# Turning B and C of eight chunk pairs on VectorE instead of TensorE, in a fused Mamba-2 and PReLU kernel

## The chip, the cores and the metric

The kernel runs on one NeuronCore of a Trainium2 chip. The metric is the device time of one execution in microseconds, the median over several runs. The core has five engines that run side by side, each through its own list of instructions in order: TensorE (PE in the profile; PEld is its loading of weights), VectorE (DVE), ScalarE (ACT), GpSimd (POOL) and SyncE (SP), which here issues most of the transfers between the main memory and the on-chip memory SBUF. Matmul results land in PSUM. An engine waits for another through semaphores.

## The reference

Two blocks follow each other. The first is a Mamba-2 state-space scan in chunks, the second a dense layer with PReLU.

```python
# x: (4, 8, 768, 32)   a: (4, 8, 768)   B, C: (4, 8, 768, 16)    float32
log_a = np.log(np.clip(a, 1e-06, 1.0))
for c in range(nc):                                  # chunks along the sequence
    cum  = np.cumsum(la, axis=-1)
    L    = np.exp(cum[:, :, :, None] - cum[:, :, None, :]) * causal
    CB   = np.einsum('bhin,bhjn->bhij', Cc, Bc)      # products of C and B
    M    = CB * L
    y_intra = np.einsum('bhij,bhjd->bhid', M, xc)
    y_inter = np.einsum('bhin,bhnd->bhid', Cc, state) * np.exp(cum)[:, :, :, None]
    y[:, :, sl] = y_intra + y_inter
    state = decay_full[:, :, None, None] * state + np.sum(Bx, axis=2)   # Bx from B, x, decay
# ...
x = attn_out.transpose(0, 2, 1, 3).reshape(3072, 256)
h = x @ w_in                                         # w_in: (256, 2048)
g = np.maximum(h, 0.0) + alpha * np.minimum(h, 0.0)
out = g @ w_out                                      # w_out: (2048, 256)
```

## The kernel before

The kernel works in chunks of Q = 128 positions, two chunks at a time: a *pair*, gp = 0 to 11. Two pairs fill a group of 512 tokens, which the dense layer then takes. The dense layer of group 1 onwards is done in *quads* of four row blocks, `quad(g, z, after)`, by a scheme of seven products with sums and differences of blocks in place of eight products. Between its steps a quad calls `after(1)` to `after(14)`, and there the parts of the next group's pairs are put in. So the state-space work of pairs 4 to 11 is spread through the matmuls of the dense layer, in an order that is fixed in the program.

Loading a pair. `nat` has B and C with positions on the partitions, and (head, state) along the row:

```python
nat = ldx.tile([P, 2, 2, H * N], F32, name="nat")
# ...
for k in range(2):
    ts = slice((c + k) * Q, (c + k + 1) * Q)
    for i, src in enumerate((B, C)):
        eng = nc.scalar if gp == 0 else nc.sync
        eng.dma_start(out=nat[:, i, k].rearrange("p (h n) -> p h n", h=H),
                      in_=src[b, :, ts, :].rearrange("h p n -> p h n"))      # L163
    nc.sync.dma_start(out=xt[:, k]..., in_=x[b, :, ts, :]...)                # L165
```

A pair's work, for the last eight pairs (`fine`, gp >= 4). The products of B and C need (head, state) on the partitions, so both are turned:

```python
# ... bn (B times decays, from nat[:, 0]), state update; yield
tp = spare() if gp == 1 else ss_tile()                       # a PSUM tile
for i in range(2):
    for k in range(2):
        nc.tensor.transpose(tp[:, (2 * i + k) * P : (2 * i + k + 1) * P], nat[:, i, k],
                            ident)                           # L511
bc = work.tile([P, 4, Q], F32, name="bc")
nc.scalar.copy(out=bc.rearrange("p i t -> p (i t)"), in_=tp) # L514
bh, ct = bc[:, :2], bc[:, 2:].rearrange("p k t -> p (k t)")
# ...
yield
for k in range(2):                   # each half_decays: two scans of 256 columns, L441
    for w in range(2):
        half_decays(k, w)
        if k == 1 and w == 1:
            spread_c()               # ScalarE: cz from ct, L526
            c_decayed()              # GpSimd: cd from ct, L529
        yield
# ... products of bh and cz (L580), times the decays (L614), y (L633, L640), copy to xT
```

A quad's steps (`first` is a group of four matmuls, L785; A and Y are PSUM tiles of a pool of two):

```python
first(A, lambda q: wi[:, q, 0, 0], b11, True)
m1 = ...; nc.scalar.copy(out=m1, in_=A)                          # L793
after(1)
first(Y, lambda q: s1[:, q], t1, True)
m5 = ...; nc.scalar.copy(out=m5, in_=Y)                          # L797
after(2); after(3)
first(A, lambda q: s2[:, q], t2)
u2 = ...; nc.scalar.copy(out=u2, in_=A)                          # L802
after(4)
nc.vector.tensor_tensor(out=Y, in0=Y, in1=u2, op=ALU.add)        # L804
after(5)
first(A, lambda q: wi[:, q, 1, 0], t3)
c22 = ...; nc.vector.tensor_tensor(out=c22, in0=A, in1=m5, op=ALU.add)   # L808
after(6)
first(Y, lambda q: s4[:, q], b22)          # accumulates on what L804 left in Y
prelu(g12, Y, z, 0)                        # ScalarE multiply L768, VectorE L770
prelu(g22, c22, z, 1, (nc.scalar,))
nc.scalar.copy(out=Y, in_=m1)                                    # L814
prelu(g22, c22, z, 1, (nc.vector,))
after(7); after(8)
# ... g21 from A
first(Y, lambda q: wi[:, q, 0, 1], b21)
prelu(g11, Y, z, 0)                        # the quad's last PReLU
# ... GpSimd differences of the g blocks, L828
after(11); after(12); after(13); after(14)
```

A pair's turning of B and C is called at `after(12)` of an odd quad (z = 1 or 3), its first two scans at `after(14)`, the next four at `after(1)` and `after(2)` of the following quad, and the last two at its `after(5)`. Pair 4 alone has its first parts, the turning and two scans among them, ahead of the first quad. From group 2 on, `after(11)` of an odd quad has `finish`, which turns one half of the output of the group before with a VectorE block transpose (L904) and stores it. The products with `w_out` (L760; in the first quads also L699) stand between the steps.

Of the kernel before, what the change touches and what calls it, by code (L numbers as in the profile page):

```python
# [9 lines left out]
F32 = mybir.dt.float32  # L10
# [12 lines left out]
def kernel(  # L23
# [25 lines left out]
    nc = tc.nc  # L49
# [4 lines left out]
    batch, H, S, D = x.shape  # L54
    N = B.shape[-1]
    P = 128
    Q = 128
# [8 lines left out]
    GC = 4  # L66
# [20 lines left out]
    ldx = ctx.enter_context(tc.tile_pool(name="ldx", bufs=3))  # L87
# [5 lines left out]
    gp = ctx.enter_context(tc.tile_pool(name="gp", bufs=16))  # L93
# [6 lines left out]
    def bank(i):  # L100


        return ps_q.tile([P, 512], F32, name="bank", tag=f"q{i}")
# [5 lines left out]
    def ss_tile():  # L109
        if early[0] is None:  # L110
            return ps_s.tile([P, 512], F32, name="ss")
        early[0] += 1
        i = early[0] % (3 if ident_p else 4)
        return ps_s.tile([P, 512], F32, name="ss") if i < 2 else bank(i)
# [4 lines left out]
    def load_rows(i):  # L119

        rows = ld.tile([RW, Q], F32, name="rows")
        nc.sync.dma_start(out=rows, in_=a.rearrange("b h (c t) -> (b h c) t", t=Q)[i * RW : (i + 1) * RW])
        loads["r", i] = rows
# [3 lines left out]
    def load_a(t, b, c, eng=nc.sync):  # L127
        first = a[b, 0:1, c * Q : (c + 2) * Q]
        eng.dma_start(out=t, in_=bass.AP(tensor=first.tensor, offset=first.offset,
                                             ap=[[S, H], [0, N], [1, 2 * Q]]))  # L130

    def load_spread(gp, b, c):

        for k, t in enumerate(loads["p", gp][1]):
            rows = scratch["z", b // 2].rearrange("(b h c) t -> b c h t", b=2, h=H)[b % 2, c + k]
            nc.sync.dma_start(out=t.rearrange("p (h t) -> p h t", h=H),
                              in_=rows.unsqueeze(0).to_broadcast([P, H, Q]))

    def load_pair(gp, decays=True):


        b, c = divmod(2 * gp, CPB)
        nat = ldx.tile([P, 2, 2, H * N], F32, name="nat")
        xt = ldx.tile([P, 2, HD], F32, name="xt")

        ap = ldx.tile([P, 2 * Q], F32, name="ap")
        if gp == 0:
            load_a(ap, b, c, nc.scalar)
        elif gp >= NB:
            rows = scratch["pf", b // 2].rearrange("(b h c) t -> b h (c t)", b=2, h=H)  # L150
            rows = rows[b % 2, :, c * Q : (c + 2) * Q]
            nc.sync.dma_start(out=ap, in_=rows.unsqueeze(1).to_broadcast([H, N, 2 * Q]))
        if gp == 0:
            load_rows(0)
            nc.sync.dma_start(out=al_n, in_=moe_alpha.rearrange("(k p) -> k p", p=P))
            loads["a", 1] = prep.tile([P, 2 * Q], F32, name="a1")
            load_a(loads["a", 1], b, c + 2)
        abc = []
        for k in range(2):
            ts = slice((c + k) * Q, (c + k + 1) * Q)  # L160
            for i, src in enumerate((B, C)):
                eng = nc.scalar if gp == 0 else nc.sync
                eng.dma_start(out=nat[:, i, k].rearrange("p (h n) -> p h n", h=H),  # L163
                              in_=src[b, :, ts, :].rearrange("h p n -> p h n"))
            nc.sync.dma_start(out=xt[:, k].rearrange("p (h d) -> p h d", h=H),  # L165
                              in_=x[b, :, ts, :].rearrange("h p d -> p h d"))
        for k in range(2 if gp >= NB else 0):
            abc.append(lda.tile([P, H * Q], F32, name="abc"))
        loads["p", gp] = nat, abc, xt, ap
        if decays:  # L170
            load_spread(gp, b, c)
# [6 lines left out]

    al_n = const.tile([NF, P], F32, name="al_n")
    load_pair(0)  # L180

    w_in = const.tile([P, KC, d_ff], F32, name="w_in")
# [84 lines left out]
    def keep_warm(to, n, cols=2 * Q):  # L267

        for i in range(n):
            nc.tensor.matmul(to[:, :cols], warm[:, :P], warm[:, :cols], start=True, stop=True,  # L270
                             skip_group_check=True)

    keep_warm(ps_h.tile([P, GT], F32, name="hp"), 7, Q)
    ident = const.tile([P, P], F32, name="ident")
# [3 lines left out]
                          in_=ident.unsqueeze(1).to_broadcast([P, H, Q]))  # L278
# [135 lines left out]
    def spare():  # L414

        return ps_h.tile([P, GT], F32, name="hp", tag="hp")

    def pair(gp):

        b, c = divmod(2 * gp, CPB)  # L420
        nat, abc, xt, ap = loads["p", gp]
        last = c + 2 == CPB
        fine = gp >= 2 * GC // 2
# [79 lines left out]
            yield  # L503


        tp = spare() if gp == 1 else ss_tile()
        if gp == 0:
            keep_warm(tp, 3, Q)
        for i in range(2):
            for k in range(2):  # L510
                nc.tensor.transpose(tp[:, (2 * i + k) * P : (2 * i + k + 1) * P], nat[:, i, k],  # L511
                                    ident)
        bc = work.tile([P, 4, Q], F32, name="bc")
        nc.scalar.copy(out=bc.rearrange("p i t -> p (i t)"), in_=tp)  # L514
        bh, ct = bc[:, :2], bc[:, 2:].rearrange("p k t -> p (k t)")
        cz = czp.tile([P, 2, 2, Q], F32, name="cz")
        cd = work.tile([P, 2, Q], F32, name="cd")
# [130 lines left out]
        for w in range(KC):  # L648
            nc.scalar.copy(out=xts[g][:, w, q * Q : (q + 2) * Q],
                           in_=y[w].rearrange("p k t -> p (k t)"))  # L650
# [266 lines left out]
    def ssm(gp, stages=1):  # L917

        if gp not in pairs:
            pairs[gp] = pair(gp)  # L920
        for i in range(stages):
            next(pairs[gp], None)
# [27 lines left out]
    held["pr"] = rows_scan(0)  # L950
    rows_out(0)
    load_pair(1)
    load_second()
    load_next(2)
    load_pair(2, False)
    load_next(2)
    load_spread(2, *divmod(4, CPB))
# [153 lines left out]
```

## Time and profile before

| | before |
|---|---|
| median of 3 runs | 373.09 us (372.91 to 373.69) |
| span in the profile | 371.6 us |
| TensorE busy | 363.5 us, 98% |
| VectorE busy | 246.2 us, 66% |
| ScalarE busy | 180.1 us, 48% |
| GpSimd busy | 201.5 us, 54% |
| mean granted TensorE clock | 1.000 |
| the chain that ended last | PE 83%, DVE 9%, DMA 3%, ACT 2% |

The page gives each engine's busy time, a picture of the span in 40 slices, the chain of work that ended last (followed back from the last instruction to what released each step), and groups of instructions by their line in the kernel. A row of a group reads: line, engine, operation, written tile <- read tiles, shape, count | busy time in us, mean ns of one | idle time of the engine just before, and what ended it. The trace behind the page can be asked for a timeline, in which equal neighbours are merged: start, length, instruction, number of them. Matmuls are pipelined and each one's length includes its way through the array, so the time that a group takes is read from the distance between starts.

### The profile page before, as it was taken

To read this page: it belongs to the slowest core of one execution; us is meant where nothing else is said; L and a number is where in the kernel's file an instruction comes from. 1 tells how busy PE (TensorE), PEld (TensorE's weight loads), DVE (VectorE), ACT (ScalarE), POOL (GpSimd) and SP (SyncE) were. 2 spreads that over 40 slices of the span, in tenths; PEclk is the share of its full clock that TensorE was granted. 3 is DMA by queue.
4 is the path that set the end of the run, shared out by engine and by line. 5 is a ranking of instruction groups with operands and counts; after the bars stand their busy time and mean duration, and the time that the engine had idled before them with its cause. 6 is when DMAs were issued, how large, how long until landed. Compare 5 with 4: busy or idle time off the path is not lost.

```text
span 371.6 us, 6171 instructions
## 1 busy us (share of the span) xinstructions
PE 363.5 (98%) x2223; PEld 291.6 (78%) x2223; DVE 246.2 (66%) x462; ACT 180.1 (48%) x384; POOL 201.5 (54%) x211
## 2 busy tenths in 40 slices
PE   8989999999999999999999999999999999999996
PEld 7766666578788888788788788788788788888884
DVE  7897979968548647838638738638747644643364
ACT  1647866426345345444445445436436425553541
POOL 4875565779738845625636526437445345264512
PEclk9999999999999999999999999999999999999999
DMA  7889999911084401004603702801801001001004
GB/s 148 182 172 321 264 261 203 190 39 58 29 156 100 84 3 56 2 0 64 149 3 57 156 2 44 171 0 30 175 10 29 2 0 25 6 0 30 0 0 85
DMA packets 121877, 30.71 MB, mean 83 GB/s; under 512 B 93736, under 2 KB 117752, under 8 KB 121848
## 3 DMA queue, kind: packets, MB, share of 16 engines
q1 hardware_dynamic: 116736, 29.74, 35.9%
q10 hardware_dynamic: 5112, 0.59, 1.1%
q8 instruction: 17, 0.28, 0.3%
q14 instruction: 12, 0.10, 0.1%
HBM read 26.98 MB, written 3.34 MB: 82 GB/s over the span
## 4 chain that ended last, share of the span: by engine, by line
PE 83%; DVE 9%; DMA 3%; ACT 2%; issue 1%; ACTq 1%; POOLq 0%; SPq 0%; DVEq 0%
PE hp L785 34%; PE bank L760 32%; PE bank L699 3%; PE hp L661 2%; PE ss L640 2%; PE ss L580 2%; DVE dec L441 2%; DMA rows<-in_a_dram 2%; PE ss L633 1%; DVE wr L239 1%; DMA nat<-in_B_dram 1%; DVE dec L435 1%; PE ss L478 1%; PE hp L676 1%; PE ss L511 1%
## 5 line engine op out<-in xcount | busy, mean ns | idle before, releaser
L828 POOL TENSOR_TENSOR gt<-gt 128x512 f32<-128x512 f32 x58 | 73.8, 1272 | 38.3 <-DVE gt L770 31.6
L760 PE MATMUL bank<-gt,w_out 128*128 128x256 f32 x320 | 82.4, 381 | 0.0
L770 DVE SCALAR_TENSOR_TENSOR gt<-hp,s_mul,gt 128x256 f32<-128x256 f32 x120 | 52.4, 478 | 43.5 <-ACT gt L768 40.8
L768 ACT ACTIVATE gt<-hp,s_alpha 128x256 f32<-128x256 f32 x120 | 50.4, 471 | 48.7 <-PE hp L785 36.5
L760 PEld LDWEIGHTS bank<-gt,w_out 128*128 128x128 f32 x320 | 60.1, 190 | 10.4 <-issue 2.3
L760 PE MATMUL bank<-gt,ws 128*128 128x256 f32 x240 | 59.5, 379 | 0.0
L819 POOL TENSOR_TENSOR gt<-gt 128x512 f32<-128x512 f32 x20 | 25.4, 1272 | 56.9 <-DVE gt L770 56.5
L760 PEld LDWEIGHTS bank<-gt,ws 128*128 128x128 f32 x240 | 45.1, 190 | 5.8
L441 DVE TENSOR_TENSOR_SCAN dec<-abc,bank 128x256 f32<-128x256 f32 x80 | 48.0, 659 | 0.0
L785 PE MATMUL hp<-xs,w_in 128*128 128x256 f32 x160 | 42.3, 387 | 0.0
L785 PE MATMUL hp<-xT,w_in 128*128 128x256 f32 x160 | 41.9, 384 | 0.1
L785 PE MATMUL hp<-xs,ws 128*128 128x256 f32 x160 | 40.7, 382 | 0.0
L793 ACT COPY m<-hp 128x512 f32<-128x512 f32 x20 | 11.7, 586 | 52.5 <-PE hp L785 47.4
L804 DVE TENSOR_TENSOR hp<-hp,u 128x512 f32<-128x512 f32 x20 | 13.8, 692 | 34.5 <-ACT u L802 34.5
L785 PEld LDWEIGHTS hp<-xT,w_in 128*128 128x128 f32 x160 | 29.1, 190 | 7.2 <-ACT hp L814 2.9
L785 PEld LDWEIGHTS hp<-xs,ws 128*128 128x128 f32 x160 | 29.8, 190 | 5.5 <-issue 1.1
L785 PEld LDWEIGHTS hp<-xs,w_in 128*128 128x128 f32 x160 | 29.3, 190 | 6.1 <-issue 1.2
L699 PE MATMUL bank<-w_out,gt 128*128 128x256 f32 x128 | 31.0, 384 | 0.0
L699 PEld LDWEIGHTS bank<-w_out,gt 128*128 128x128 f32 x128 | 23.7, 190 | 6.6 <-issue 3.7
L493 POOL TENSOR_TENSOR sm<-state,bmask 128x256 f32<-128x256 f32 (+1 forms) x12 | 8.0, 663 | 34.8 <-DVE state L490 34.6
L661 PE MATMUL hp<-xT,w_in 128*128 128x512 f32 x48 | 22.8, 597 | 0.6 <-DVE gt L665 0.3
L770 DVE SCALAR_TENSOR_TENSOR gt<-c,s_mul,gt 128x256 f32<-128x256 f32 x40 | 20.8, 560 | 0.0
(156 smaller groups left out, 548.8 us busy)
## 6 DMA issues: line engine op xcount, KB each, us to landing
abc<-z SPq DMA_DIRECT2D x20, 512.0 KB, 5.1
raw<-in_moe_w_in_dram SPq DMA_DIRECT2D x8, 512.0 KB, 5.5
raw<-in_moe_w_out_dram SPq DMA_DIRECT2D x8, 512.0 KB, 6.9
xt<-in_x_dram SPq DMA_DIRECT2D x24, 128.0 KB, 3.1
out_dram<-o_sb SPq DMA_DIRECT2D x32, 64.0 KB, 1.9
nat<-in_B_dram SPq DMA_DIRECT2D x22, 64.0 KB, 3.3
nat<-in_C_dram SPq DMA_DIRECT2D x22, 64.0 KB, 2.8
ap<-pf SPq DMA_DIRECT2D x11, 128.0 KB
```

The costliest lines, as they stand in the source:

```text
L441: nc.vector.tensor_tensor_scan(out=dv[:, k, hs], data0=abc[k][:, hs], data1=ident_p[0], initial=0.0, op0=ALU.mult, op1=ALU.add)
L493: nc.gpsimd.tensor_tensor(out=sm[:, :nk], in0=new[:, :nk], in1=hmask.unsqueeze(1).to_broadcast([P, nk, P]), op=ALU.mult)
L661: nc.tensor.matmul(hp, w_in[:, k, f * P : (f + 1) * P], xts[g][:, k], start=(k == 0), stop=(k == KC - 1))
L699: nc.tensor.matmul(pos[0][t // 2][:, t % 2], gt[:, t * Q : (t + 1) * Q], w_out[:, f], start=(f == 0 and t % 2 == 0), stop=(f == NF - 1), s ...
L760: nc.tensor.matmul(ms[g][i][:, h], w, blocks[g, z][n][:, p], start=(q == 0 and h == 0), stop=(q == NQ - 1), skip_group_check=True)
L768: nc.scalar.mul(o[:, p], h[:, p], s_alpha[:, fs[p]])
L770: nc.vector.scalar_tensor_tensor(out=o[:, p], in0=h[:, p], scalar=s_mul[:, fs[p]], in1=o[:, p], op0=ALU.mult, op1=ALU.max)
L785: nc.tensor.matmul(to[:, p], w(2 * z + p), b, start=start and p == 0, stop=True, skip_group_check=True)
L793: nc.scalar.copy(out=m1, in_=A)
L804: nc.vector.tensor_tensor(out=Y, in0=Y, in1=u2, op=ALU.add)
L819: nc.gpsimd.tensor_tensor(out=tc_, in0=g22, in1=g12, op=ALU.subtract)
L828: eng.tensor_tensor(out=o, in0=x0, in1=x1, op=ALU.subtract)
```

## The change

For the last eight pairs the turning of B and C is taken from TensorE. Their B and C are loaded a second time (C only in this way) so that a partition holds eight neighbouring positions of one head, 128 floats in a run: partition 32 j + s of `nat[:, 1 + e, i]` has positions 8 s to 8 s + 7 of head 2 j + e. A 32x32 block of this, with the 32 partitions of j on one side and the two heads' 16 states of one position on the other, has as its transpose 32 rows (head, state) and 32 positions that are 8 apart. One VectorE instruction turns all 64 blocks and writes each position where it belongs in `bc`, with a step of 8 floats. The four TensorE transposes, the PSUM tile and the ScalarE copy of these pairs go. The purpose is to take work from TensorE, the busiest engine. The first four pairs stay as they were.

```diff
-        nat = ldx.tile([P, 2, 2, H * N], F32, name="nat")
+        turned = gp >= GC
+        nat = ldx.tile([P, 3, 2, H * N], F32, name="nat")
# ...
-            for i, src in enumerate((B, C)):
+            for i, src in enumerate((B,) if turned else (B, C)):
# ...
+        for i, src in enumerate((B, C) if turned else ()):
+            for e in range(2):
+                first = src[b, e : e + 1, c * Q : (c + 2) * Q, :]
+                nc.sync.dma_start(out=nat[:, 1 + e, i],
+                                  in_=bass.AP(tensor=first.tensor, offset=first.offset,
+                                              ap=[[2 * S * N, P // 32], [8 * N, 32], [1, 8 * N]]))
# ...
-        tp = spare() if gp == 1 else ss_tile()
-        if gp == 0:
-            keep_warm(tp, 3, Q)
-        for i in range(2):
-            for k in range(2):
-                nc.tensor.transpose(tp[:, (2 * i + k) * P : (2 * i + k + 1) * P], nat[:, i, k],
-                                    ident)
         bc = work.tile([P, 4, Q], F32, name="bc")
-        nc.scalar.copy(out=bc.rearrange("p i t -> p (i t)"), in_=tp)
+        if fine:
+            nc.vector.transpose(
+                bc.rearrange("p (i k) t -> p i (k t)", i=2).rearrange("p i (c b) -> p i b c", b=8),
+                nat[:, 1:].rearrange("p e i (b n) -> p (i b) e n", n=N))
+        else:
+            # the transposes and the copy as before
```

More of the change, by code (lines that the diff above doesn't have):

```diff
@@ L503, in pair @@
             yield
-        tp = spare() if gp == 1 else ss_tile()
-        if gp == 0:
-            keep_warm(tp, 3, Q)
-        for i in range(2):
-            for k in range(2):
-                nc.tensor.transpose(tp[:, (2 * i + k) * P : (2 * i + k + 1) * P], nat[:, i, k],
-                                    ident)
-        bc = work.tile([P, 4, Q], F32, name="bc")
-        nc.scalar.copy(out=bc.rearrange("p i t -> p (i t)"), in_=tp)
+        bc = work.tile([P, 4, Q], F32, name="bc")
+        if fine:
[3 more added lines that the diff above has]
+        else:
+            tp = spare() if gp == 1 else ss_tile()
+            if gp == 0:
+                keep_warm(tp, 3, Q)
+            for i in range(2):
+                for k in range(2):
+                    nc.tensor.transpose(tp[:, (2 * i + k) * P : (2 * i + k + 1) * P],
+                                        nat[:, i, k], ident)
+            nc.scalar.copy(out=bc.rearrange("p i t -> p (i t)"), in_=tp)
         bh, ct = bc[:, :2], bc[:, 2:].rearrange("p k t -> p (k t)")
```

## The prediction

> **What bounds the kernel now.** I read the page first, for which engine is full; then the chain of work that ended last; then the groups of instructions, for the price of the transposes, the copy and a VectorE transpose; and last the timeline around one pair's transposes, because an average cannot say which wait ends last there. The page's busy line:
>
> ```profile
> PE 363.5 (98%) x2223; PEld 291.6 (78%) x2223; DVE 246.2 (66%) x462; ACT 180.1 (48%) x384; POOL 201.5 (54%) x211
> ```
>
> TensorE (PE) is busy 98% of the span, at a mean granted clock of 1.000; the chain gives PE 83%. VectorE (DVE) at 66% seems to have room to take work over. That is the argument for the change, and I do not trust it: 66% is a mean over stretches with different limits. The groups, shapes apart (columns: instructions | busy us, mean ns | idle before):
>
> ```profile
> L511 PE MATMUL ss<-ident,nat 128*128 128x128 f32 x36 | 5.5, 276 | 0.0
> L514 ACT COPY bc<-ss 128x512 f32<-128x512 f32 x9 | 5.3, 588 | 2.3 <-PE ss L511 2.2
> L904 DVE STREAM_TRANSPOSE o_sb<-c 128x512 f32<-128x512 f32 x8 | 5.6, 700 | 0.0
> L904 DVE STREAM_TRANSPOSE o_sb<-c 128x256 f32<-128x256 f32 x1 | 0.4, 445 | 0.0
> ```
>
> L511 are the transposes to go, L514 their copy, and L904 is VectorE's block transpose of the same 128x512 size, which the kernel already uses to turn outputs: 700 ns. Now the timeline at pair 7 (columns: start us, length us, engine, line). VectorE:
>
> ```profile
> 169.21 0.88 DVE L770 SCALAR_TENSOR_TENSOR gt<-hp,s_mul,gt 128x256 f32<-128x256 f32 x2 [0.78 <-ACT gt L768]
> 170.00 0.70 DVE L904 STREAM_TRANSPOSE o_sb<-c 128x512 f32<-128x512 f32 x1
> 170.62 3.54 DVE L441 TENSOR_TENSOR_SCAN dec<-abc,bank 128x256 f32<-128x256 f32 x6
> 174.09 0.67 DVE L804 TENSOR_TENSOR hp<-hp,u 128x512 f32<-128x512 f32 x1
> 174.67 1.25 DVE L441 TENSOR_TENSOR_SCAN dec<-abc,bank 128x256 f32<-128x256 f32 x2
> ```
>
> and TensorE, with the weight load (PEld) of the matmuls that follow L804:
>
> ```profile
> 168.07 0.60 PE L511 MATMUL ss<-ident,nat 128*128 128x128 f32 x4
> 168.51 1.03 PE L760 MATMUL bank<-gt,ws 128*128 128x256 f32 x4
> ...
> 174.20 1.03 PE L785 MATMUL hp<-xs,w_in 128*128 128x256 f32 x4
> 174.85 0.84 PEld L785 LDWEIGHTS hp<-xT,ws 128*128 128x128 f32 x4
> 175.07 1.03 PE L785 MATMUL hp<-xT,ws 128*128 128x256 f32 x4
> ```
>
> From 169.21 to 174.76 VectorE has no gap: the PReLU of the quad's last block, the output transpose, six decay scans, then L804, which adds u2 to PSUM tile Y. The next matmuls into Y (`first(Y, s4, b22)`) accumulate on top and must wait for it. Their weight load starts at 174.85, only 0.09 us after L804 ends at 174.09 + 0.67 = 174.76. So at this point VectorE is within 0.09 us of being what TensorE waits for.
>
> **What the Trainium skill says.** "TensorE: Matmul & The Clock Gate", Part 4 (PE-mode transpose), gives about 275 ns for a transpose in a kernel's context; the trace has 276 ns, but they are pipelined and I use start distances. "VectorE: DVE Perf Modes", The three transpose paths, says VectorE turns 32x32 blocks only; this is why B and C must be loaded in another layout, and L904 shows the same operation. "Advanced Engine Details and Errata", SBUF Cachelines: lines are 16 bytes, and accesses that each go to another line are slower. The new transpose writes tokens with a step of 8 floats, 32 bytes; L904 writes contiguously, so no run here shows such a write. "DMA: Bandwidth & Descriptors", Specifications, wants 512 bytes or more for full rate; the page counts 93736 of 121877 packets under 512 bytes.
>
> **The change part by part.**
> - Removed from TensorE: four transposes per pair. In the trace they begin at 168.07 and the next group at 168.51; groups of four 128x256 matmuls step by 0.866. I take 0.435 us per pair, 8 x 0.435 = 3.5 us. This much, 0.9%, would be gained if nothing else moved.
> - Removed from ScalarE: 8 x 0.588 = 4.7 us of copies. After each, ScalarE idles (1.65 us before the next L793 at pair 7): worth nothing.
> - Added to VectorE: one 128x512 transpose per pair. The compared instruction orders put it directly before the six scans (behind the output transpose in pairs 7 to 11), nothing else moves. L904 starts at 170.00 and the scan at 170.62, so a step is 0.62 us, 8 x 0.62 = 5.0 us. It stands in exactly the gapless stretch above.
> - DMA: two loads of C in 64-byte runs per pair become four of 64 KB in 512-byte runs; B's old loads stay for `bn`. This is 1024 x 2 packets fewer, 128 x 4 more. The DMA engines are busy 20 to 41% from 150 to 250 us, and B's second load is issued earlier since C no longer stands between. Worth 0.
> - PSUM: the tile for the transposes goes, so the two-slot pool alternates evenly. Each slot's earlier reader is done long before.
>
> Net per pair: let m be the weight load's start less L804's end in the kernel before. L804 moves 0.62 later, the weight load would like to be 0.435 earlier. A released load starts about 0.05 after its releaser (L814 ends at 150.18, PEld at 150.23), and a stalled group loses 0.11 less than its load's delay (next group 0.97 after the load, against 0.215 + 0.866 = 1.08 in flow). Delay against before = 0.62 + 0.05 - 0.11 - m = 0.56 - m. The saved 0.435 cancels, as the end of the chain is then VectorE's.
> - Pairs 7 to 11, read in the same way from the timeline (load less end of L804): 174.85 - 174.76, 203.35 - 203.19, 232.06 - 231.96, 260.55 - 260.39, 289.05 - 288.95, so m = 0.09, 0.16, 0.10, 0.16, 0.10 and the delays are 0.47, 0.40, 0.46, 0.40, 0.46: +2.19 us.
> - Pairs 5 and 6 have no output transpose. L804 has 0.23 idle before it (it waits for ScalarE's u2 copy); operations overlap by about 0.05, so it moves 0.62 - 0.23 - 0.05 = 0.34. m = 117.67 - 117.24 and 146.37 - 145.94, both 0.43; 0.34 + 0.05 - 0.11 - 0.43 = -0.15 each.
> - Pair 4 has 0.51 idle: L804 moves 0.06; m = 87.92 - 87.78 = 0.14; 0.06 - 0.06 - 0.14 = -0.14.
>
> Sum 2.19 - 0.44 = +1.75, giving 374.8 us. Nothing later absorbs it: the next chain (Y's matmuls, ScalarE's multiply, VectorE's PReLU, ScalarE's copy L814, the next matmuls into Y) starts from the very matmuls that are late, and TensorE already waits at its end, by the table of waits (us in total, times, longest):
>
> ```profile
> PEld hp L785 <- ACT hp L814: 2.9, 8, 0.4
> ```
>
> **The rivals.**
> 1. TensorE's saving comes through. For it: PE 98%, VectorE 66%. Time 373.1 - 3.5 = 369.6. Against it: the gapless VectorE stretch and margins of 0.09 to 0.16 us. It needs the transpose to finish in a gap of VectorE, which the in-order stream has not.
> 2. The strided write slows the transpose. From 445 ns at 256 columns and 700 at 512, streaming costs about 1 ns a column and 190 ns are fixed. If the 32-byte step halves the streaming, a transpose takes about 1.21 us, 0.51 more; nearly all is exposed, in pairs 4 to 6 too, as their stall has begun: 8 x 0.51 = 4.1 more, 378.9 us. For it: the page on cachelines. Against: no strided VectorE write in this trace; a read with an 8-byte step (L238, 701 ns) costs as much as the contiguous L904. I give it four in ten.
> 3. A late load: the transpose waits for four more DMAs. Pair 8's loads are issued at 172.8 to 177.9 and used at 196.5, so 18 us remain against about 3 us of landing. Worth 0, unless the abc loads behind them come late; they are needed at 199.
>
> **Range and chances.** Predicted is 375.6 us, between 374.8 (six in ten) and 378.9 (four in ten), nearer the likelier. The range 373.0 to 380.0 takes in a cheaper wake-up or a smaller exposed part below and the slow write above. Faster by 2% (365.6) is more than all the transposes cost: 0.02. Slower by 2% starts at 380.6 and needs a transpose above some 1.4 us or a second effect: 0.07. Within 2%: 0.91.
>
> **What would show it.** In the changed profile the new transposes at about 700 ns (step 2: 1200); a new entry "PEld hp <- DVE hp" among the waits, some 0.9 us for each of pairs 7 to 11 and 0.3 for pairs 4 to 6; PE busy about 3 us lower while the period between pairs, 28.5 us, is not shorter. I am wrong if that wait is missing and TensorE runs on at 0.866 us per group there.

## The result, and the profile after

| | before | after |
|---|---|---|
| median | 373.32 us (372.91 to 373.69, 4 runs) | 376.94 us (376.33 to 377.41, 4 runs) |
| ratio of the times | 1 | 1.0093, 95% interval 1.0075 to 1.011 |
| span in the profile | 371.6 us | 374.4 us |

The changed kernel is 0.9% slower: 3.5 us. The prediction was 375.6 us with a range of 373.0 to 380.0, and 0.91 on "within 2%". The page of the kernel after begins with the busy line, and its chain of work that ended last with the shares by engine:

```profile
PE 362.2 (97%) x2191; PEld 288.0 (77%) x2191; DVE 252.5 (67%) x470; ACT 175.7 (47%) x376; POOL 201.6 (54%) x211
...
PE 76%; DVE 14%; issue 3%; ACT 2%; DMA 2%; SPq 2%; ACTq 0%; POOL 0%; POOLq 0%; DVEq 0%
```

TensorE has 32 instructions fewer and 1.3 us less busy time, VectorE 8 more and 6.3 us more. The two move little; what moves is the path. VectorE's share of the chain goes from 9% to 14% and TensorE's from 83% to 76%: there are now more places where the end is set by VectorE. The groups of the kernel after, shapes apart, give the price of the new instruction (L517) beside that of the output transpose (L918, which was L904 before):

```profile
L918 DVE STREAM_TRANSPOSE o_sb<-c 128x512 f32<-128x512 f32 x8 | 5.6, 702 | 0.0
L517 DVE STREAM_TRANSPOSE bc<-nat 128x512 f32<-128x512 f32 x8 | 8.7, 1089 | 0.0
```

Operation, shape and type are the same, yet the new one takes 1089 ns against 702. Now the waits of the kernel after (engine, what is written, line <- releaser: us in total, times, longest). L799 are the matmuls of `first` (before L785), L818 is the add of u2 into Y (before L804), L828 is the ScalarE copy into Y (before L814):

```profile
PEld hp L799 <- DVE hp L818: 8.4, 8, 1.3
PEld hp L799 <- ACT hp L828: 2.9, 8, 0.4
```

The second entry stands as before. The first is new: eight times, once in each of the changed pairs, the weight load that follows the add of u2 waits for it. Where this comes from is seen in the timeline at pair 7, VectorE of the kernel after:

```profile
168.45 0.88 DVE L784 SCALAR_TENSOR_TENSOR gt<-hp,s_mul,gt 128x256 f32<-128x256 f32 x2 [0.78 <-ACT gt L782]
169.24 0.70 DVE L918 STREAM_TRANSPOSE o_sb<-c 128x512 f32<-128x512 f32 x1
169.87 1.08 DVE L517 STREAM_TRANSPOSE bc<-nat 128x512 f32<-128x512 f32 x1
170.79 3.51 DVE L450 TENSOR_TENSOR_SCAN dec<-abc,bank 128x256 f32<-128x256 f32 x6
174.23 0.67 DVE L818 TENSOR_TENSOR hp<-hp,u 128x512 f32<-128x512 f32 x1
```

and TensorE with its weight loads there:

```profile
174.95 0.73 PEld L799 LDWEIGHTS hp<-xT,ws 128*128 128x128 f32 x4 [1.32 <-DVE hp L818]
174.95 1.13 PE L799 MATMUL hp<-xT,ws 128*128 128x256 f32 x4 [0.92 <-DVE hp L818]
```

The transpose stands in VectorE's list between the output transpose and the six scans, and from 168.45 to 174.90 VectorE has no gap. From the start of the output transpose to the end of the add it took 4.76 us before (170.00 to 174.76) and takes 5.66 now (169.24 to 174.90): 0.90 more, nearly all of the 0.92 between the starts of L517 and the first scan. The weight load starts 0.05 after the add ends, having idled 1.32 us.

How much of that the end sees is read from the start of each pair's first y product, taken as a mark in both timelines. The first stage, whose pairs are turned as before, ended 0.92 us earlier in the profile of after. That is scatter: over the profiles of all kernels here its end lies between 73.9 and 75.7 us, with the old loads (74.0 to 75.2) as with the new ones (73.9 to 75.7). It is the first column, and each later pair's own delay is the step to the next column:

| mark of pair | 3 | 4 | 5 | 6 | 7 | 8 | 9 | 10 | 11 |
|---|---|---|---|---|---|---|---|---|---|
| before, us | 74.85 | 102.65 | 131.13 | 159.91 | 188.34 | 216.89 | 245.54 | 274.09 | 302.53 |
| after, us | 73.93 | 101.74 | 130.28 | 159.15 | 188.32 | 217.56 | 246.96 | 276.19 | 305.37 |
| after less before | -0.92 | -0.91 | -0.85 | -0.76 | -0.02 | 0.67 | 1.42 | 2.10 | 2.84 |
| the pair's own delay | | 0.01 | 0.06 | 0.09 | 0.74 | 0.69 | 0.75 | 0.68 | 0.74 |

Pairs 7 to 11 lose 3.60 us, pairs 4 to 6 lose 0.16; 3.76 in all, against 3.5 measured. This is the whole loss, and nearly all of it lies where the output transpose and the new transpose stand one behind the other.

### The profile page after: what moved, and what is told of

Its sections match the earlier page's. It is cut to its first block, busy times and chain, and to the rows that moved or that the text cites. A ratio compares the mean times of both kernels' runs of the same rounds, so it can differ in the third digit from the quotient of the medians.

```text
span 374.4 us, 6125 instructions
## 1 busy us (share of the span) xinstructions
PE 362.2 (97%) x2191; PEld 288.0 (77%) x2191; DVE 252.5 (67%) x470; ACT 175.7 (47%) x376; POOL 201.6 (54%) x211
## 4 chain that ended last, share of the span: by engine, by line
PE 76%; DVE 14%; issue 3%; ACT 2%; DMA 2%; SPq 2%; ACTq 0%; POOL 0%; POOLq 0%; DVEq 0%
PE bank L774 27%; PE hp L799 26%; DVE dec L450 7%; PE bank L713 7%; PE hp L675 6%; PE ss L654 2%; PE ss L594 2%; ACT gt L782 2%; DVE bc L517 2%; PE ss L647 1%; DVE gt L784 1%; PE ss L487 1%; DVE hp L818 1%; DMA nat<-in_C_dram 1%; PE hp L690 1%
## 5 line engine op out<-in xcount | busy, mean ns | idle before, releaser
L799 PE MATMUL hp<-xs,w_in 128*128 128x256 f32 x160 | 42.3, 387 | 0.0
L799 PE MATMUL hp<-xT,w_in 128*128 128x256 f32 x160 | 42.0, 385 | 0.1
L799 PE MATMUL hp<-xs,ws 128*128 128x256 f32 x160 | 40.7, 382 | 0.0
L818 DVE TENSOR_TENSOR hp<-hp,u 128x512 f32<-128x512 f32 x20 | 13.8, 688 | 33.5 <-ACT u L816 33.5
L799 PEld LDWEIGHTS hp<-xT,w_in 128*128 128x128 f32 x160 | 29.1, 190 | 7.4 <-ACT hp L828 2.9
L799 PEld LDWEIGHTS hp<-xs,ws 128*128 128x128 f32 x160 | 29.8, 190 | 5.5 <-POOL gt L842 1.1
L799 PEld LDWEIGHTS hp<-xs,w_in 128*128 128x128 f32 x160 | 29.3, 190 | 6.1 <-issue 1.5
L799 PE MATMUL hp<-xT,ws 128*128 128x256 f32 x80 | 21.4, 389 | 5.2 <-DVE hp L818 5.2
```

What stands on the lines that cost most here:

```text
L799: nc.tensor.matmul(to[:, p], w(2 * z + p), b, start=start and p == 0, stop=True, skip_group_check=True)
```

## The experiments

The theory: the transpose lengthens an in-order VectorE stretch whose end TensorE was already within 0.1 us of waiting for, so what TensorE saves is lost in a wait, and the write with a step of 32 bytes makes the transpose longer still. Rivals: the new loads cost the time; the read of the new layout, not the write, makes the transpose slow; TensorE's saving is there, and something else costs more than it.

**1. No turning at all** (kernel before). In pairs 4 to 11 nothing is turned and nothing copied; the products of B and C read a constant tile, so this leaves out the part of the computation whose place is in question.

```diff
-        tp = spare() if gp == 1 else ss_tile()
-        # ... four transposes, copy to bc
+        if fine:
+            bc = no_bc                    # a constant tile
+        else:
+            # ... as before
```

> The kernel before with the turning of B and C left out for pairs 4 to 11 (no TensorE transposes, no ScalarE copy, no VectorE transpose; the products read a constant tile instead, so the output is not the reference's). It bounds what the removal alone can bring. Theory (VectorE's chain takes back what TensorE saves): with nothing added to VectorE the whole 8 x 0.435 = 3.5 us appears: 373.3 - 3.5 = 369.8 us, ratio 0.991, and no wait of TensorE for L804. Rival (the transposes were hidden anyway, under other waits of TensorE): about 373 us.

Measured 371.96 us, ratio 0.9954 (0.9931 to 0.9977): 1.7 us gained, not the 3.5 that all TensorE transposes take. The waits show what holds the rest back (here L790 are the matmuls of `first`, L809 the add of u2):

```profile
PEld hp L790 <- DVE hp L809: 2.0, 5, 0.4
```

The expectation missed this. Five times, in pairs 7 to 11, the wait is there with these pairs turned on no engine. The reason is in the prediction's own numbers: m, the room that the weight load had before, is 0.09 to 0.16 us in those pairs. TensorE comes 0.435 earlier and meets the add, which the output transpose ahead of it delays. The prediction's sum with no new transpose, 0 + 0.05 - 0.11 - m, gives -0.15 to -0.22 for each of these five, -0.9 together, and -0.435 for each of pairs 4 to 6, -1.3: in all -2.2, inside the interval (-2.6 to -0.9). The marks of this kernel bear out the five: their steps are 0.15, 0.21, 0.15, 0.21 and 0.16 us shorter than before. Pairs 4 to 6 take off 0.63, 0.01 and 0.44, 1.1 together and not 1.3. Pair 5's saving is lost at its products of B and C, which take 1.54 us from their start to the next group (123.50 to 125.04) where they took 1.11 before (124.64 to 125.75); pair 4's products take 1.71 (94.00 to 95.71) where they took 1.95 (94.46 to 96.41). So even a free transpose, in this order, was worth about half of what TensorE saves.

**2. Both** (kernel after). The VectorE transpose stays and four TensorE transposes a pair are put back, into a tile that nobody reads. They stand for the old work; no copy follows.

```diff
         if fine:
+            tp = ss_tile()
+            for i in range(2):
+                for k in range(2):
+                    nc.tensor.transpose(tp[:, ...], nat[:, 0, k], ident)
             nc.vector.transpose(
```

> The changed kernel with the four TensorE transposes per pair put back at their place (they read the naturally loaded B twice; nobody reads their result, and there is no ScalarE copy); VectorE turns as in the changed kernel. Theory: each of the eight pairs ends in TensorE's wait for VectorE, about 1 us long, so 0.435 us more of TensorE work ahead of it vanishes in the wait: 376.9 us, the same as the changed kernel, and the wait for the VectorE add shrinks from 8.4 us to about 5. Rival (the costs of the engines add up, or the change's cost lies elsewhere, in loads or PSUM tiles): 376.9 + 3.5 = 380.4 us.

Measured 376.78 us, 1.0076 (1.0048 to 1.0104); the interval holds the ratio of after. Doing the TensorE transposes as well costs nothing. The wait of that kernel (L804 `first`, L823 the add):

```profile
PEld hp L804 <- DVE hp L823: 5.0, 8, 0.9
```

It shrinks from 8.4 to 5.0 us, 3.4 for eight pairs, nearly the 3.5 us of transposes. This shows that in the changed kernel TensorE's saving is real and is spent on waiting. The rival in which the engines' costs add up would have had this kernel at 380.4 us.

**3. The loads alone** (kernel before, with the loads of after). The old turning stays, but since C is no longer loaded in the old layout, it turns B twice, so the result is that of other data with the same work.

```diff
-            for i, src in enumerate((B, C)):
+            for i, src in enumerate((B,) if turned else (B, C)):
+        for i, src in enumerate((B, C) if turned else ()):
+            # ... the block loads of the changed kernel
...
-                    nc.tensor.transpose(..., nat[:, i, k], ident)
+                    nc.tensor.transpose(..., nat[:, 0, k], ident)
```

> The changed kernel's loads (B twice, C only in blocks, the larger tile) with the old turning: four TensorE transposes and the ScalarE copy, which read the naturally loaded B in place of C too, so the output is not the reference's. VectorE has no new work. Theory: the loads are hidden; 373.3 us, ratio 1.000. Rival (the four more transfers per pair, or their order in the queue, cost the time): 375 to 377 us.

Measured 372.92 us, 0.998 (0.9968 to 0.9992). The loads cost nothing; if anything they save a little, 0.3 to 1.2 us. The rival of the loads falls.

**4. Contiguous write** (kernel after). Each block is written to 32 neighbouring columns. The instruction has the same size; the positions land permuted, so the products are of permuted positions.

```diff
-                bc.rearrange("p (i k) t -> p i (k t)", i=2).rearrange("p i (c b) -> p i b c", b=8),
+                bc.rearrange("p (i k) t -> p i (k t)", i=2).rearrange("p i (b c) -> p i b c", b=8),
```

> The changed kernel with the VectorE transpose writing its 32 positions of a block side by side instead of 8 floats apart (positions land permuted, so the output is not the reference's; the reading is as in the changed kernel). Theory (the 32-byte write step is what makes the new transpose 1.08 us instead of 0.70): 0.70 us each; 0.37 us less on the path of each of the eight pairs: 376.9 - 3.0 = 373.9, and by the prediction's sum for 0.62 us a step 374.8: 373.6 to 374.9 us. Rival (the reading in runs of 16 floats, or the wait ahead of it, makes it long): 1.08 us still, 376.9 us.

Measured 374.62 us, 1.0031 (1.0022 to 1.0041). The group of the transpose and, from the waits, the entry of the add:

```profile
L517 DVE STREAM_TRANSPOSE bc<-nat 128x512 f32<-128x512 f32 x8 | 5.5, 683 | 0.0
...
PEld hp L799 <- DVE hp L818: 6.0, 8, 1.0
```

683 ns against 1089: the step of the write costs 0.41 us in each transpose, and 2.3 us of the kernel's time, 0.29 a pair. VectorE at pair 7 of this kernel shows why it is not 0.41:

```profile
169.37 0.67 DVE L517 STREAM_TRANSPOSE bc<-nat 128x512 f32<-128x512 f32 x1
169.96 3.54 DVE L450 TENSOR_TENSOR_SCAN dec<-abc,bank 128x256 f32<-128x256 f32 x6
```

The scans start 0.59 us after the transpose, where after has 0.92: only 0.33 of the length is seen by what follows. What is left, 1.2 us slower than before (0.8 to 1.5 by the interval), is what the mechanism costs with the duration that the prediction first took. Its sum for that, 1.75, is above this. By the marks of this kernel pairs 7 to 11 lose 2.10 us, as good as the predicted 2.19; pairs 4 to 6 gain 0.81 where 0.44 was predicted, and the difference lies at pair 4 (0.58 gained, 0.14 predicted).

**5. Contiguous read** (kernel after, a single run). The strided write stays, the input is read in order of address; the blocks hold other elements than the products need.

```diff
-                nat[:, 1:].rearrange("p e i (b n) -> p (i b) e n", n=N))
+                nat[:, 1:].rearrange("p e i (b m) -> p (e i b) m", m=2 * N))
```

> The changed kernel with the VectorE transpose reading each 32 columns in one run instead of two runs of 16 floats (heads and positions land mixed, so the output is not the reference's); the write keeps its step of 8 floats. Theory (the write step is slow): still about 1.08 us each, 376.9 us. Rival (the split reading is slow): 0.70 us each, about 374.5 us.

377.05 us, and the group of the transpose:

```profile
L517 DVE STREAM_TRANSPOSE bc<-nat 128x512 f32<-128x512 f32 x8 | 8.8, 1095 | 0.0
```

1095 ns, as with the split read. Reading in runs of 16 floats costs nothing here, nor beside the contiguous write (683 ns in experiment 4, against 702 for the output transpose); the write alone is slow. The rival of the read falls.

**6. The transpose twice** (kernel after). Each VectorE transpose is issued twice, into the same tile, to see whether VectorE's time comes through in full once the wait is there.

```diff
             nc.vector.transpose(bc..., nat[:, 1:]...)
+            nc.vector.transpose(bc..., nat[:, 1:]...)
```

> The changed kernel with each VectorE transpose issued twice in a row. Theory: all of a second transpose lies on the path, 8 x 0.97 = 7.8 us: 384.7 us, and TensorE's wait for the VectorE add grows from 8.4 to about 16 us. Rival (the cost of the change lies elsewhere, or VectorE has slack that takes more work): clearly less, 377 to 381 us.

388.28 us, 1.0402 (1.0376 to 1.0428), 11.3 us over after and 3.6 over what was expected. The wait (L802 `first`, L821 the add):

```profile
PEld hp L802 <- DVE hp L821: 17.7, 8, 2.5
```

It grows by 9.3 us, 1.16 a pair. VectorE at pair 7:

```profile
174.55 1.08 DVE L517 STREAM_TRANSPOSE bc<-nat 128x512 f32<-128x512 f32 x1
175.67 1.13 DVE L520 STREAM_TRANSPOSE bc<-nat 128x512 f32<-128x512 f32 x1
176.63 3.52 DVE L450 TENSOR_TENSOR_SCAN dec<-abc,bank 128x256 f32<-128x256 f32 x6
```

The second transpose starts 1.12 us after the first, not 0.92 as the scans did. VectorE's time does come through in full. About 1.4 us more come once in this execution, behind pair 8's stall. TensorE there, then each engine's busy time and the granted clock (the column 0.56, 0.72) in two stretches of this kernel:

```profile
211.15 1.88 PE L802 MATMUL hp<-xT,ws 128*128 128x256 f32 x4 [2.02 <-DVE hp L821]
```

```profile
211.10:213.30 2.20, 2.15 (x6) 1.69 (x7) 1.74 (x3) 0.19 (x1) 0.00 (x0) 0.56 0.55 101
213.30:216.00 2.70, 2.70 (x11) 2.26 (x10) 1.73 (x5) 2.33 (x6) 0.22 (x1) 0.72 0.71 213
```

After 2.02 us of idleness the group of four took 1.88 us in place of 1.13. In slices of 1 us the clock is 0.50 from 212 to 214 and 1.00 again from 215. Stalls of 2.08 us at pairs 7 and 9 lowered no clock. What set this one apart stays open. The other executions of this kernel differ too: the one with the highest mean clock, 0.998, took 386.82 us, 9.9 over after and close to the growth of the wait; the one with the lowest, 0.990, took 389.65.

**7. The transpose moved** (kernel after). If the place is what costs, the same instruction elsewhere must be cheap. It depends on loads alone, so it can stand anywhere behind them. In a quad VectorE waits for ScalarE's copy of u2 before the add: in the waits of the kernel after this is 33.5 us over 12 quads. The transposes of pairs 5 to 11 are put ahead of that add, in the odd quad before (its `after(3)`), some 12 us earlier.

```diff
+    def turn_early(gp):
+        turned_bc[gp] = work.tile([P, 4, Q], F32, name="bc")
+        turn_pair(loads["p", gp][0], turned_bc[gp])
...
-        bc = work.tile([P, 4, Q], F32, name="bc")
+        bc = turned_bc.pop(gp) if gp in turned_bc else work.tile([P, 4, Q], F32, name="bc")
...
+            early = nxt + {(1, 3): 1, (3, 3): 2}.get((z, j), NP)
+            if early < NP:
+                turn_early(early)
```

> The changed kernel with the VectorE transposes of pairs 5 to 11 issued some 10 us earlier, in the odd quad's step 3 ahead of the add of u2, where VectorE idles 1.98 to 3.95 us in the kernel before; pair 4's stays. Theory: there the transpose is hidden, the scans start as early as in the kernel before, and TensorE keeps its saving in seven pairs, 7 x 0.435 = 3.05, while pair 4 costs about 0.2: 370.5 us, ratio 0.992, with the wait for the VectorE add gone but for pair 4. Rival (VectorE's 5 to 8 us of added work costs wherever it is put, or the earlier transpose waits for its loads): 374 to 377 us.

371.91 us, 0.9964 (0.9951 to 0.9977): the same instruction with the same duration, and 5.0 us less than after. The change now gains 0.4% over before. The expected 370.5 is not reached: a wait of 2.6 us in six places stays, pair 4's and, as in experiment 1, those of the output transposes. Pair 5's saving is missing too, again as in experiment 1: from pair 4's mark to its own it takes 28.48 us, as before.

**8. Pair 4's moved too** (kernel 7). Its transpose goes ahead of the last part of the dense layer's first group.

```diff
-    early_turn = set(range(5, NP))
+    early_turn = set(range(4, NP))
...
+        if f == NF - 1:
+            turn_early(4)
         hidden(0, f)
```

> As the run before, and pair 4's transpose too is moved ahead, before the last PReLU of the first group's sixteen blocks, where VectorE idles 1.93 us. Theory: 373.3 - 3.5 = 369.8 us, ratio 0.991, the same as with no turning at all. Rival: the transpose of pair 4 delays the first group instead, 370.5 us or more.

371.14 us, 0.994 (0.9928 to 0.9953). The waits of this kernel (L810 `first`, L829 the add):

```profile
PEld hp L810 <- DVE hp L829: 2.0, 5, 0.4
```

These are the same 2.0 us, five times, as in the kernel with no turning at all, and the intervals of the two times overlap. The new transposes are now free; what is left belongs to the output transposes.

**9. The output transposes moved** (kernel 8). `finish` goes from `after(11)` to `after(3)` of the same odd quad, into the same idle time.

```diff
-            if g > 1 and z in (1, 3) and j == 11:
-                finish(g - 1, z // 2)
...
                 turn_early(early)
+            if g > 1 and z in (1, 3) and j == 3:
+                finish(g - 1, z // 2)
```

> As the run with pair 4's transpose moved too, and the output transposes of the groups before (5 of them before the scans of pairs 7 to 11) moved as well, from the end of the odd quad to its step 3, behind the new transpose. Theory: what was left there, TensorE waiting 0.4 us for the VectorE add in each of pairs 7 to 11 (2.0 us in total, some 1.4 us of it lost), is the output transpose's doing, as its 0.62 us made the margin 0.09 to 0.16 us; with both out of the way the wait is gone and 8 x 0.435 = 3.5 us come through: 373.3 - 3.5 = 369.8 us, ratio 0.991. Rival (the two transposes together, 1.6 us, overfill the gap of 1.98 us, or that wait was not on the path): 371.1 us or more, as without the second move.

371.26 us, 0.9938 (0.9926 to 0.9951), nothing gained over 8. In the timeline of this kernel, in the last group, VectorE and the weight load:

```profile
326.25 0.71 DVE L929 STREAM_TRANSPOSE o_sb<-c 128x512 f32<-128x512 f32 x1 [3.17 <-POOL c L880]
```

```profile
327.61 0.73 PEld L810 LDWEIGHTS hp<-xT,ws 128*128 128x128 f32 x4 [1.44 <-DVE hp L829]
```

The five waits are gone, but in the last group, where no pair's work stands between, GpSimd's sum (L880) that the output transpose reads is not ready. VectorE, in order, waits 3.17 us for it with the add behind it, and TensorE waits 1.44 for the add. The old place had its reason there.

**10. The output transposes alone moved** (kernel before).

```diff
-            if g > 1 and z in (1, 3) and j == 11:
+            if g > 1 and z in (1, 3) and j == 3:
```

> The kernel before, with only the output transposes moved in the same way; turning as before on TensorE and ScalarE. Theory: in the kernel before TensorE does not wait at that place, so freeing VectorE by 0.62 us there brings nothing: 373.3 us, ratio 1.000. Rival (the output transposes were themselves on the path, and e9's gain is theirs alone): 371.9 us or less.

374.36 us, 1.0029 (1.002 to 1.0039), with the same single wait of 1.4 us. Moving them gains nothing in the kernel before, because TensorE, still doing its transposes, did not wait for the add there, and it adds the wait in the last group.

**11. Moved, but not in the last group** (kernel 9).

```diff
-            if g > 1 and z in (1, 3) and j == 3:
+            if g > 1 and z in (1, 3) and j == (11 if g == NG - 1 else 3):
```

> As the run with the output transposes moved, but in the last group, which has no pairs and scans beside it, the output transposes stay at the end of the odd quad. Theory: the one wait of 1.4 us for the VectorE add that the move brought lies in that group (the moved output transpose there waits for GpSimd's last sums, ahead of the add); without it e9's 371.26 falls by about 1.3 to 370.0 us, ratio 0.991, the bound of 8 x 0.435 = 3.5 us less. Rival (the wait is not on the path, or the saving is limited by something else): 371.1 us or more.

369.91 us, 0.9907 (0.9892 to 0.9922): 3.5 us faster than before and 7.0 faster than the change as it was made. The kernel computes all that the reference does and is the fastest of all. By its marks pairs 6 to 11 gain 0.43 to 0.45 us each, the 0.435 of their four transposes; pairs 4 and 5 gain 0.61 and 0.04. No wait of a weight load for the add is left. VectorE's timeline, where both transposes now stand, and further on at pair 7 where they stood:

```profile
157.46 1.10 DVE L431 STREAM_TRANSPOSE bc<-nat 128x512 f32<-128x512 f32 x1
158.41 0.67 DVE L929 STREAM_TRANSPOSE o_sb<-c 128x512 f32<-128x512 f32 x1
159.52 0.70 DVE L829 TENSOR_TENSOR hp<-hp,u 128x512 f32<-128x512 f32 x1 [0.43 <-ACT u L827]
...
169.75 3.56 DVE L462 TENSOR_TENSOR_SCAN dec<-abc,bank 128x256 f32<-128x256 f32 x6
173.23 0.67 DVE L829 TENSOR_TENSOR hp<-hp,u 128x512 f32<-128x512 f32 x1
```

and TensorE with its weight loads:

```profile
174.16 0.84 PEld L810 LDWEIGHTS hp<-xT,ws 128*128 128x128 f32 x4
174.38 1.03 PE L810 MATMUL hp<-xT,ws 128*128 128x256 f32 x4
```

Both transposes end and 0.43 us of idle time (1.10 in every second such place) is still left before the add, which waits for u2 and not for them. Further on the add ends at 173.90 and the weight load at 174.16 follows the earlier loads without a wait: 0.26 us of room, where after had a wait of 1.32. The page's first line of this kernel:

```profile
PE 360.7 (98%) x2191; PEld 288.8 (78%) x2191; DVE 254.6 (69%) x470; ACT 175.8 (48%) x376; POOL 201.5 (55%) x211
```

VectorE works 2.1 us longer than in the changed kernel, 254.6 against 252.5; what makes the time is the order.

**12. The same move alone** (kernel before, with the last edit).

> The kernel before, with the output transposes moved in the same way (not in the last group); turning as before on TensorE and ScalarE. Theory: TensorE does not wait for VectorE there in the kernel before, so nothing is gained: 373.3 us, ratio 1.000, and no wait for the VectorE add. Rival (the gain of the run beside it is due to the output transposes alone): about 370 us.

373.35 us, 0.9995 (0.9986 to 1.0004). Without the turning on VectorE the move is worth nothing, so the 3.5 us of kernel 11 come from taking the turning off TensorE, and both moves only let them through.

## Why the prediction was right, by its steps

The mechanism held: VectorE's chain at the add takes back what TensorE saves. The case called likelier, a step of 0.62 us, did not come; the measured time lies between the two cases, and the range was wide enough to hold both.

- **Removed from TensorE, 3.5 us.** Right in size: experiment 2 puts 3.4 us back into the wait, and kernel 11 gains 3.5. In the changed kernel none of it reached the end, as the step "The saved 0.435 cancels" said. "PE busy about 3 us lower" was wrong: it is 1.3 lower. The stalled groups are listed longer, 1.13 us in place of 1.03 for each, which makes 0.8 of the missing 1.7; the rest is not explained.
- **Removed from ScalarE: worth nothing.** No run isolated the copy. In kernel 11, which has no copy either, pairs 6 to 11 gain what the transposes alone take on TensorE; nothing speaks for a gain from the copy.
- **Added to VectorE.** Place and mechanism were right: directly before the six scans, in the gapless stretch, and exposed behind the output transpose. The step "a step is 0.62 us" is the term that was mis-sized: 0.92 at pair 7. The prediction had it as rival 2, with four chances in ten, and oversized it there: "0.51 more" took the streaming to be halved, and "nearly all is exposed" does not hold. The trace gives 0.39 more for the length (1089 ns against 700), of which the chain to the end of the add sees 0.28 in pairs 7 to 11. The Trainium skill, "Advanced Engine Details and Errata", SBUF Cachelines, says that accesses that each go to another cacheline are slower; experiment 4 agrees for this write, 1089 against 683 ns.
- **The sum.** With 0.90 for 0.62 the prediction's formula reads 0.90 + 0.05 - 0.11 - m = 0.84 - m: 0.75, 0.68, 0.74, 0.68, 0.74 for pairs 7 to 11, against 0.74, 0.69, 0.75, 0.68, 0.74 in the table of marks. The wake-up of 0.05, the 0.11 and m hold.
- **Pairs 4 to 6.** Predicted -0.14, -0.15, -0.15; measured 0.01, 0.06, 0.09. For pairs 5 and 6 the idle time before the add took up part, as worked out, and the longer transpose the rest: the chain to the end of the add grew by 0.57 in place of 0.34, and 0.57 + 0.05 - 0.11 - 0.43 = 0.08. For pair 4 the same sum, with its chain grown by 0.29, gives 0.09. With the short transpose, for which the sum was made, experiment 4 has -0.58, -0.01 and -0.22: the sum misses what experiment 1 shows at the products of pairs 4 and 5, which take 1.57 and 1.31 us there and took 1.95 and 1.11 before.
- **What would show it.** The wait came, eight times, and longer than "0.9 us each" and "0.3": 1.25 to 1.32 in pairs 7 to 11, 0.6 to 0.7 in pairs 4 to 6. Experiment 4, with the short transpose, has 0.95 to 1.02 and 0.32 to 0.36; the 0.3 between is the longer transpose. The period between pairs is 29.2 to 29.4 us from pair 7 on, not shorter than 28.5.
- **Rival 1** fell for this order of instructions and holds for another: its gain of 3.5 us is what kernel 11 reached. **Rival 3** fell with experiment 3.
- **The range.** Over before, the two cases were 1.75 us (a transpose of 0.70) and 5.8 (1.21). Measured were 1.2 with the contiguous write (683 ns) and 3.5 with the real transpose (1089). Both costs were oversized, the first in pairs 4 to 6, the second by the halved streaming and by what of it is exposed. That 374.62 us in experiment 4 is so near to the predicted 374.8 is luck: the kernel before took 373.5 beside it and not 373.09.

## What to carry to other kernels

Before work is given to an engine that is "66% busy", read in the timeline the very place where it will stand in that engine's list: how long since its last gap, what follows it, and by how much the next consumer misses waiting. If it depends on nothing but a load, put it where that engine idles already; in this kernel the same instruction cost 3.5 us at one place and, with the output transposes moved too, let 3.5 us through at another. An order that costs nothing now can become the bound once the other engine is relieved, so the list has to be read again after each gain, and the last pass of a loop on its own.

## What was not expected of the hardware

- A 128x512 float32 block transpose on VectorE that writes with a step of 32 bytes takes 1089 ns against 683 for the contiguous write: (1089 - 683) / 512 = 0.79 ns more per column. On top of the roughly 1 ns per column of the contiguous write, (700 - 445) / 256, this is less than a halving. Reading in runs of 16 floats costs nothing (1089 and 1095 ns; with the contiguous write 683 against 702).
- A second transpose into the same tile starts 1.12 us after the first; a scan behind a transpose starts after 0.92 to 0.96.
- Once, after TensorE had idled 2.02 us, its granted clock fell to 0.50 and was back at 1.00 within 4 us; twice it idled 2.08 us in the same kernel without any loss. One execution does not tell why.
